# Normalising the FFN's residual from SBUF tiles, with new due times around it: an FNet + FFN kernel on one core

## The chip, the cores and the metric

One core of a Trainium2 chip runs the whole program. Time is device time in microseconds, the median of several executions. Engines are named as in the profile: PE (TensorE), DVE (VectorE), ACT (ScalarE), POOL (GpSimd) and SP (SyncE, whose queue issues most loads).

## The reference

```
x = A_x                                     # 1 x 2048 x 512
h = x + fnet(layernorm(x))                  # fnet: a = n @ hid_re.T, b = n @ hid_im.T
                                            #       y = seq_re @ a - seq_im @ b
h2 = h + silu(layernorm(h) @ w1) @ w2       # w1: 512 x 1792, w2: 1792 x 512
```

All in fp32, out 2048 x 512. The sequence matrices are 2048 x 2048, the hidden ones 512 x 512.

## The kernel before

Every fp32 product is made of three matmuls: each operand is split in a rounded part (ACT, `rounded`, L77) and a remainder (DVE, L81, written to `pl`, `gtl` and the like), and `three` (L123 to L125) adds high x high, high x low and low x high into PSUM. Four of the five large products are made with seven block products in place of eight; the sums and differences of blocks that this needs are DVE work (L411, `sums_h`, `sums_w1`, `sums_w2`, `sums_g`).

The stages follow each other on PE: `plain(0, 0)`, `fast(1, 0)`, `mix(0)` (first half q = 0: the two sequence products and the hidden one), then `fast(0, 1)`, `fast(1, 1)`, `mix(1)` for the half q = 1, then the FFN: `up(0)`, `down(0)`, `up(1)`, `down_fast(1)`. A stage `fast` is 28 steps of 12 matmuls, the first 12 of them on loaded blocks and the other 16 on differences of blocks (DVE: a subtraction L411 and a remainder L81 for each step). `mix(q)` is two halves (tau = 0, 1) of 96 matmuls; each half ends in `add_y` (L476), which adds the PSUM sums onto the tiles `h` with x, and `store_h` (L480), by which POOL writes these tiles to HBM (`hd`). `up` is steps of six matmuls, in the order n = 1, 7, 6, 2, 5 for p = 0 and then 1, 2, 3, 6, 4, 7, 5, with 3 and 4 of the p before. What follows a product there: a copy of Y to SBUF (ACT, L688, L692, L694), an add from the tile `vx` (DVE, L680) and SiLU (ACT, L677).

`norm_h(q, tau, start)` (L529) is the second layer norm, on transposed tiles, so that its sums run across partitions. Its parts have due times behind `start`: load of the residual from `hd` (-8, SP, L537), `mean` (0: two adds, then an all-reduce on POOL, L524 to L526), `center` (7 and 9, L545), `square` (10 and 12, ACT, L551), `var` (15, again `total`), `once` (21: POOL writes the row of variances to HBM, L557, and reads it back four to a partition, L559), `root` (29: thirteen small DVE operations from L563, then two DMAs on POOL, L565 and L568, that spread the result), `scale` (42 and 44, L573) and, for q = 0, `store` to HBM (46). For q = 0 the normalised tiles are loaded again (`load_hn`); `up` makes its moving side T from them, `lead` us before its start and after.

The order of all work is set by a planner: `step` counts PE's time in units of 0.2265 us per matmul (MM_US) and gives each piece of other work a due time before or behind a step; `at` gives one directly. At the end (L945) all pieces are sorted by due time, and PE, DVE, ACT and POOL each run theirs in that order. SP's transfers are issued in the order of the program too, each as soon as its page is free. Operands are rounded PREP_US = 8 before their step, loads are due LOAD_US = 18 before. All SBUF tiles but a few small ones are pages of 4 KB per partition, PAGES = 51 of them, taken and freed in turn; PSUM holds four tiles of two banks.

`down_fast(1)` ends the kernel: in the order of L894 the last product is n = 4 of p = 6, cut in two steps of three matmuls (L904 to L906), each followed by `post4` (an add, L850, and a store, L819).

At the start, 15 matmuls on zeros (WARM, L940) run on PE before the first operands are there.

Of the kernel before, what the change touches and what calls it, by code (L numbers as in the profile page):

```python
# [12 lines left out]
ALU = mybir.AluOpType  # L13
# [4 lines left out]
D = 512  # L18
# [6 lines left out]
NP = NF // 2  # L25
# [1 line left out]
NJ = S // P // 4  # L27
EPS = 1e-5
PAGES = 51
WARM = 15  # L30
MM_US = 0.2265
PREP_US = 8.0
LOAD_US = 18.0
# [5 lines left out]
def fnet_ffn_kernel(  # L39
# [20 lines left out]
    nc = tc.nc  # L60
# [7 lines left out]
    def page(name, dt=F32, shape=(2, 512)):  # L68
        return pages.tile([P, *shape], dt, tag="pg", name=name)
# [57 lines left out]
    events, clock = [], [0.0]  # L127

    def step(n, mm, before=(), after=()):

        t, end = clock[0], clock[0] + n * MM_US
        for lead, f in before:
            events.append((t - lead, 1, len(events), f))
        events.append((t, 2, len(events), mm))
        for delay, f in after:
            events.append((end + delay, 0, len(events), f))
        clock[0] = end

    def at(t, f):
        events.append((t, 1, len(events), f))  # L140
# [333 lines left out]
    def add_y(q, tau):  # L474
        for e in range(2):
            nc.vector.tensor_tensor(h[q, tau, e], y.pop((q, tau, e)), h[q, tau, e], op=ALU.add)  # L476

    def store_h(q, tau):
        for e in range(2):
            nc.gpsimd.dma_start(hd[q][tau, e], h.pop((q, tau, e)))  # L480

    def mix(q):
        for tau in range(2):
            for c in range(2):
                for i in range(2):

                    def round_h(c=c, i=i):
                        H[c, i], remainder = rounded(raw.pop(("H", c, i)), f"H{c}{i}")
                        return remainder

                    def round_c(tau=tau, c=c, i=i):
                        key = "M", q, tau, c, i
                        part[key], remainder = rounded(C.pop((c, q, i, tau)), "p", -1.0 if c else 1.0)
                        return remainder

                    def mm(tau=tau, c=c, i=i):
                        hi, lo = part.pop(("M", q, tau, c, i))
                        wh, wl = H[c, i] if tau == 0 else H.pop((c, i))
                        for e in range(4):
                            if c == 0 and i == 0 and e % 2 == 0:  # L500
                                y[q, tau, e // 2] = banks(f"y{q}{tau}{e}")
                            for m in range(2):
                                s = slice(e * P, (e + 1) * P)
                                three(y[q, tau, e // 2][:, e % 2, :], wh[:, m, s], wl[:, m, s], hi[:, m, :], lo[:, m, :],
                                      c == 0 and i == 0 and m == 0, c == 1 and i == 1 and m == 1)

                    before, after = halves(PREP_US, round_c), []
                    if tau == 0:
                        before = [(LOAD_US, lambda c=c, i=i: load_hid(c, i)), *halves(PREP_US, round_h)] + before
                    if c == 0:  # L510
                        before.append((LOAD_US - 1, lambda i=i, tau=tau: load_c(q, i, tau)))
                    if c == 1 and i == 0:
                        before.append((LOAD_US, lambda tau=tau: load_h(q, tau)))
                    if c == 1 and i == 1:
                        after = [(0, lambda tau=tau: add_y(q, tau)), (6, lambda tau=tau: store_h(q, tau))]
                    step(24, mm, before, after)

    hn = {}
    nd = dram.tile([2, 2, P, 2, 512], F32, name="nd")

    def total(a, b, name):

        t = page(name)
        nc.vector.tensor_tensor(t, a, b, op=ALU.add)  # L524
        nc.vector.tensor_tensor(t[:, 0, :], t[:, 0, :], t[:, 1, :], op=ALU.add)
        nc.gpsimd.partition_all_reduce(t[:, 1, :], t[:, 0, :], channels=P, reduce_op=REDUCE_ADD)  # L526
        return t

    def norm_h(q, tau, start):  # L529

        ln, sq = {}, {}
        token = [dram.tile([512], F32, name=f"tk{q}{tau}{n}") for n in range(2)]

        def load():
            for e in range(2):
                ln[e] = page(f"hr{q}{tau}{e}")
                nc.sync.dma_start(ln[e], hd[q][tau, e])  # L537

        def mean():
            ln["m"] = total(ln[0], ln[1], f"m{q}{tau}")  # L540

        def center(e):
            m = ln["m"]
            for n in range(2):
                nc.vector.scalar_tensor_tensor(  # L545
                    ln[e][:, n, :], m[:, 1, :], -1.0 / D, ln[e][:, n, :], op0=ALU.mult, op1=ALU.add
                )

        def square(e):
            sq[e] = page(f"sq{q}{tau}{e}")  # L550
            nc.scalar.activation(sq[e], ln[e], AF.Square)  # L551

        def var():
            ln["v"] = total(sq.pop(0), sq.pop(1), f"v{q}{tau}")

        def once():
            nc.gpsimd.dma_start(token[0], ln.pop("v")[0:1, 1, :])  # L557
            ln["w"] = small.tile([P, 4, 4], F32, name="rs2")
            nc.gpsimd.dma_start(ln["w"][:, 0, :], token[0].rearrange("(p j) -> p j", j=4))  # L559

        def root():
            v, _, _, b = w = [ln["w"][:, n, :] for n in range(4)]
            nc.vector.tensor_scalar(v, v, 1.0 / D, EPS, op0=ALU.mult, op1=ALU.add)  # L563
            guessed(*w)
            nc.gpsimd.dma_start(token[1].rearrange("(p j) -> p j", j=4), b)  # L565
            ln.pop("w")
            ln["r"] = page(f"r{q}{tau}")
            nc.gpsimd.dma_start(ln["r"][:, 0, :], token[1].partition_broadcast(P))  # L568

        def scale(e):  # L570
            v = ln.pop(e)
            for n in range(2):
                nc.vector.tensor_tensor(v[:, n, :], v[:, n, :], ln["r"][:, 0, :], op=ALU.mult)  # L573
            hn[q, e, tau] = v

        def store():
            for e in range(2):
                nc.gpsimd.dma_start(nd[tau, e], hn.pop((q, e, tau)))

        for d, f in ((-8, load), (0, mean), (7, lambda: center(0)), (9, lambda: center(1)),  # L580
                     (10, lambda: square(0)), (12, lambda: square(1)), (15, var), (21, once),
                     (29, root), (42, lambda: scale(0)), (44, lambda: scale(1))):
            at(start + d, f)
        if q == 0:
            at(start + 46, store)
# [224 lines left out]
    def down_fast(q):  # L810
# [29 lines left out]
        def mul(n, p, ms=(0, 1)):  # L840
            if p == 0:
                bank[n] = banks(f"f{n}")
            w, b = {1: (U, 0), 2: (U, 1), 3: (U, 2), 5: (V, 0), 6: (V, 1), 7: (V, 2), 4: (V, 3)}[n]
            (wh, wl), (hi, lo) = w[p], mov[n, p]
            for m in ms:
                s = slice(m * P, (m + 1) * P)
                three(bank[n][:, m, :], wh[:, b, s], wl[:, b, s], hi, lo, p == 0, p == NP - 1)
# [26 lines left out]
        def post4(m):  # L874
            add(r[1, 0][:, m, :], bank[4][:, m, :], r[1, 0][:, m, :])
            store(1, 0, m)
# [19 lines left out]
        for n, p in order:  # L896
            before, after = [], []
            if n == 6:
                before.append((LOAD_US, lambda p=p: fetch_w2(p, V, 2)))
            if n == 6 and p in (2, 3):  # L900
                before.append((LOAD_US - 1, lambda k=(1, p - 2): load_r(*k)))
            if p == NP - 1:
                after = [(0, {6: post6, 7: post7, 5: post5, 4: None}[n])]
            if n == 4 and p == NP - 1:  # L904
                for m in range(2):
                    step(3, lambda m=m: mul(4, NP - 1, (m,)), before, [(0, lambda m=m: post4(m))])  # L906
            else:
                step(6, lambda n=n, p=p: mul(n, p), before, after)

    plain(0, 0)  # L910
    for p, t in enumerate((-12, -5, 61, 68, 94, 102, 110)):
        sums_w1(clock[0] + t, p)
    fast(1, 0)
    mix(0)
    norm_h(0, 0, clock[0] - 3)
    fast(0, 1)
    norm_h(0, 1, clock[0] + 8)
    fast(1, 1)
    mix(1)
    for k in range(2):  # L920
        for tau in range(2):
            at(clock[0] - 40 + 2 * k + tau, lambda k=k, tau=tau: load_hn(k, tau))
    second = down(0), down_fast(1)
    norm_h(1, 0, clock[0] - 4)
    norm_h(1, 1, clock[0] + 15)
    up(0, 28, lambda: next(second[0]))
    list(second[0])
    up(1, 24, lambda: next(second[1]))
    list(second[1])

    warm = keep.tile([P, 512], BF16, name="warm")
# [56 lines left out]
```

## Time and profile before

| | |
|---|---|
| time, median of 3 runs | 696.88 us (696.87 to 696.95) |
| the profiled execution's own time | 696.81 us |
| its span, first to last instruction | 695.0 us |
| PE busy | 687.7 us, 3009 matmuls |
| DVE busy | 520.0 us, 666 instructions |
| ACT busy | 321.4 us, 400 instructions |
| POOL busy | 80.3 us, 99 instructions |
| moved by DMA | 160.21 MB, mean 231 GB/s |

In the rows of the timeline that follow below the columns are: start, busy time (both us), engine, line, operation, written tile <- read tiles, sizes, count, and in brackets the engine's idle time before the instruction with what ended it. A row with a count over one merges instructions that follow each other. In the waits, three numbers follow the names: us in total, times, the longest. Engine names with a q are the sequencers, which issue DMAs. Rows of DMA issues end in the KB of each and the median us from issue to landing.

### The profile page before, as it was taken

What the parts mean: (1) busy time and instruction counts of PE and PEld (TensorE: products, weight loads), DVE (VectorE), ACT (ScalarE), POOL (GpSimd) and SP (SyncE); (2) the same over time, 40 slices, a digit from 0 to 9 for tenths busy, and PEclk for the clock granted to TensorE, in tenths of its full rate; (3) what the DMA queues carried; (4) which work ended last, traced back from release to release, by engine and by line L of the source; (5) the groups of instructions that cost most, each with busy time, mean ns of one, the idle gap of its engine ahead of it and who ended that gap; (6) DMA issues with size and microseconds to landing.
All of it is one profiled execution on the core that took longest, in us unless ns stands there. A gap on an engine that the chain in (4) does not pass through costs nothing.

```text
span 695.0 us, 8349 instructions
## 1 busy us (share of the span) xinstructions
PE 687.7 (99%) x3009; PEld 563.3 (81%) x3009; DVE 520.0 (75%) x666; ACT 321.4 (46%) x400; POOL 80.3 (12%) x99
## 2 busy tenths in 40 slices
PE   9999999999999999999999999999999999999996
PEld 5788888888888888888888888887888888888885
DVE  6588975987867799899989786758797233349975
ACT  4655755434233643544364126565573045565420
POOL 1011020001013200022000023311230000000000
PEclk9999999999999999999999999999999999999999
DMA  8814369467779859687893468436996195378432
GB/s 326 309 61 156 128 219 389 168 227 235 239 236 369 333 186 339 249 299 269 282 330 123 141 219 299 129 108 206 369 407 257 35 337 215 117 267 290 121 140 91
DMA packets 54136, 160.21 MB, mean 231 GB/s; under 512 B 5968, under 2 KB 13136, under 8 KB 54096
## 3 DMA queue, kind: packets, MB, share of 16 engines
q1 hardware_dynamic: 44464, 126.11, 51.7%
q0 software_dynamic: 9632, 33.58, 12.7%
q8 instruction: 23, 0.38, 0.2%
q14 instruction: 17, 0.14, 0.1%
HBM read 122.95 MB, written 36.72 MB: 230 GB/s over the span
## 4 chain that ended last, share of the span: by engine, by line
PE 93%; DVE 3%; ACT 2%; issue 1%; DMA 0%; POOL 0%
PE m L125 11%; PE m L123 11%; PE m L124 11%; PE y L123 8%; PE y L124 8%; PE y L125 8%; PE o L124 4%; PE o L123 4%; PE o L125 4%; PE f L123 3%; PE f L125 3%; PE f L124 3%; PE c L123 3%; PE c L125 3%; PE c L124 3%; PE vx L124 2%
## 5 line engine op out<-in xcount | busy, mean ns | idle before, releaser
L77 ACT ACTIVATE ph<-raw 128x1024 fp32r<-128x1024 f32 x98 | 101.8, 1057 | 100.9 <-DVE raw L411 64.4
L81 DVE TENSOR_TENSOR pl<-raw,ph 128x1024 fp32r<-128x1024 f32 x98 | 122.3, 1260 | 23.8 <-ACT ph L77 14.0
L123 PE MATMUL m<-ph,S 128*128 128x512 f32 x192 | 74.7, 389 | 0.0
L125 PE MATMUL m<-ph,S 128*128 128x512 f32 x192 | 74.7, 389 | 0.0
L124 PE MATMUL m<-pl,S 128*128 128x512 f32 x192 | 74.7, 389 | 0.0
L411 DVE TENSOR_TENSOR raw<-raw,raw 128x1024 f32<-128x1024 f32 x48 | 60.4, 1258 | 5.3 <-DMA raw<-in_seq 5.3
L123 PE MATMUL m<-ph,X 128*128 128x512 f32 x144 | 56.0, 389 | 0.0
L124 PE MATMUL m<-pl,X 128*128 128x512 f32 x144 | 56.0, 389 | 0.0
L125 PE MATMUL m<-ph,X 128*128 128x512 f32 x144 | 56.0, 389 | 0.0
L680 DVE TENSOR_TENSOR g<-vx,cp 128x512 f32<-128x512 f32 x28 | 19.3, 689 | 39.2 <-PE vx L125 33.1
L123 PE MATMUL c<-ph,X 128*128 128x512 f32 x112 | 43.6, 391 | 0.2 <-ACT X L213 0.2
L124 PE MATMUL c<-pl,X 128*128 128x512 f32 x112 | 43.7, 390 | 0.0
L125 PE MATMUL c<-ph,X 128*128 128x512 f32 x112 | 43.6, 389 | 0.0
L124 PEld LDWEIGHTS m<-pl,S 128*128 128x128 f32 x192 | 36.0, 188 | 7.6
L125 PEld LDWEIGHTS m<-ph,S 128*128 128x128 f32 x192 | 36.0, 188 | 7.5
L123 PEld LDWEIGHTS m<-ph,S 128*128 128x128 f32 x192 | 36.0, 188 | 7.4
L677 ACT ACTIVATE g<-g 128x512 f32<-128x512 f32 x42 | 26.3, 627 | 17.4 <-DVE g L680 17.4
L123 PE MATMUL f<-gth,wf 128*128 128x512 f32 x84 | 32.9, 392 | 0.8 <-DVE r L850 0.8
L77 ACT ACTIVATE gth<-g 128x1024 fp32r<-128x1024 f32 x21 | 22.1, 1057 | 23.2 <-DVE g L838 20.7
L125 PE MATMUL f<-gth,wf 128*128 128x512 f32 x84 | 32.7, 389 | 0.0
L124 PE MATMUL f<-gtl,wf 128*128 128x512 f32 x84 | 32.7, 389 | 0.0
L123 PE MATMUL o<-ph,Uh 128*128 128x512 f32 x84 | 32.7, 389 | 0.0
(273 smaller groups left out, 1583.1 us busy)
## 6 DMA issues: line engine op xcount, KB each, us to landing
raw<-in_seq SPq DMA_DIRECT2D x98, 512.0 KB, 5.9
sf<-sd SPq DMA_DIRECT2D x28, 512.0 KB, 7.2
wf<-wd SPq DMA_DIRECT2D x28, 512.0 KB, 4.5
w<-in_ffn SPq DMA_DIRECT2D x28, 256.0 KB, 5.1
hid<-in_hid SPq DMA_DIRECT2D x8, 512.0 KB, 5.1
c<-cd SPq DMA_DIRECT2D x8, 512.0 KB, 4.9
h<-in_xT SPq DMA_DIRECT2D x8, 512.0 KB, 5.7
hd<-h POOLq DMA_DIRECT2D x8, 512.0 KB, 5.6
```

The costliest lines, as they stand in the source:

```text
L77: nc.scalar.activation(hi, src, AF.Copy, scale=sign)
L81: nc.vector.tensor_tensor(lo, src, hi, op=ALU.subtract)
L123: nc.tensor.matmul(acc, wh, mh, start=first, stop=False, skip_group_check=on)
L124: nc.tensor.matmul(acc, wh, ml, start=False, stop=False, skip_group_check=on)
L125: nc.tensor.matmul(acc, wl, mh, start=False, stop=last, skip_group_check=on)
L411: nc.vector.tensor_tensor(o, a, b, op=ALU.subtract)
L677: nc.scalar.activation(g[q, f][:, tau, :], src, AF.Silu)
L680: nc.vector.tensor_tensor(g[q, f][:, tau, :], src, other, op=ALU.add)
```

## The change

1. `norm_h` loses its load. Its mean and its centering read the tiles `h` in which `add_y` made the sum; the centering writes new pages. `store_h` keeps the tiles (the end of the kernel still reads `hd`) and is due 0.5 behind `add_y` instead of 6.
2. `norm_h(q, tau)` is called at the end of each half of `mix(q)`, with `start` 2 us behind that half. Before, the starts were: (0, 0) 3 us ahead of the end of `mix(0)`, (0, 1) 8 us behind the end of `fast(0, 1)`, (1, 0) 4 us ahead of and (1, 1) 15 us behind the end of `mix(1)`.
3. The moving side T of the first FFN layer is made with a lead of 44 and 64 us instead of 28 and 24, its loads 60 us ahead of the end of `mix(1)` instead of 40. The seven `sums_w1` have other times.
4. The last product is one step of six matmuls, with both `post4` behind it.
5. WARM is 13 instead of 15.

```diff
-WARM = 15
+WARM = 13
...
     def store_h(q, tau):
         for e in range(2):
-            nc.gpsimd.dma_start(hd[q][tau, e], h.pop((q, tau, e)))
+            nc.gpsimd.dma_start(hd[q][tau, e], h[q, tau, e])
...
                     if c == 1 and i == 1:
-                        after = [(0, lambda tau=tau: add_y(q, tau)), (6, lambda tau=tau: store_h(q, tau))]
+                        after = [(0, lambda tau=tau: add_y(q, tau)), (0.5, lambda tau=tau: store_h(q, tau))]
                     step(24, mm, before, after)
+            norm_h(q, tau, clock[0] + 2)
...
-        def load():
-            for e in range(2):
-                ln[e] = page(f"hr{q}{tau}{e}")
-                nc.sync.dma_start(ln[e], hd[q][tau, e])
-
         def mean():
-            ln["m"] = total(ln[0], ln[1], f"m{q}{tau}")
+            ln["m"] = total(h[q, tau, 0], h[q, tau, 1], f"m{q}{tau}")

         def center(e):
-            m = ln["m"]
+            src, m = h.pop((q, tau, e)), ln["m"]
+            ln[e] = page(f"hr{q}{tau}{e}")
             for n in range(2):
                 nc.vector.scalar_tensor_tensor(
-                    ln[e][:, n, :], m[:, 1, :], -1.0 / D, ln[e][:, n, :], op0=ALU.mult, op1=ALU.add
+                    ln[e][:, n, :], m[:, 1, :], -1.0 / D, src[:, n, :], op0=ALU.mult, op1=ALU.add
                 )
...
-        for d, f in ((-8, load), (0, mean), (7, lambda: center(0)), (9, lambda: center(1)),
+        for d, f in ((0, mean), (7, lambda: center(0)), (9, lambda: center(1)),
...
             if p == NP - 1:
-                after = [(0, {6: post6, 7: post7, 5: post5, 4: None}[n])]
-            if n == 4 and p == NP - 1:
-                for m in range(2):
-                    step(3, lambda m=m: mul(4, NP - 1, (m,)), before, [(0, lambda m=m: post4(m))])
-            else:
-                step(6, lambda n=n, p=p: mul(n, p), before, after)
+                after = [(0, {6: post6, 7: post7, 5: post5}.get(n))]
+                if n == 4:
+                    after = [(0, lambda m=m: post4(m)) for m in range(2)]
+            step(6, lambda n=n, p=p: mul(n, p), before, after)

     plain(0, 0)
-    for p, t in enumerate((-12, -5, 61, 68, 94, 102, 110)):
+    for p, t in enumerate((-24, -12, -5, 30, 61, 68, 88)):
         sums_w1(clock[0] + t, p)
     fast(1, 0)
     mix(0)
-    norm_h(0, 0, clock[0] - 3)
     fast(0, 1)
-    norm_h(0, 1, clock[0] + 8)
     fast(1, 1)
     mix(1)
     for k in range(2):
         for tau in range(2):
-            at(clock[0] - 40 + 2 * k + tau, lambda k=k, tau=tau: load_hn(k, tau))
+            at(clock[0] - 60 + 2 * k + tau, lambda k=k, tau=tau: load_hn(k, tau))
     second = down(0), down_fast(1)
-    norm_h(1, 0, clock[0] - 4)
-    norm_h(1, 1, clock[0] + 15)
-    up(0, 28, lambda: next(second[0]))
+    up(0, 44, lambda: next(second[0]))
     list(second[0])
-    up(1, 24, lambda: next(second[1]))
+    up(1, 64, lambda: next(second[1]))
     list(second[1])
```

## The prediction

> **What bounds the kernel now.** I read the page first, then the waits of TensorE (PE), then the timeline of every engine around each place where PE waits.
>
> ```profile
> span 695.0 us, 8349 instructions
> PE 687.7 (99%) x3009; PEld 563.3 (81%) x3009; DVE 520.0 (75%) x666; ACT 321.4 (46%) x400; POOL 80.3 (12%) x99
> ```
>
> PE is busy all the time, so only its pace and its few gaps count. These are all its waits on work of the kernel (times: total, count, longest); the row after them is the wait of SP's queue that the change takes away:
>
> ```profile
> PE f L123 <- DVE r L850: 0.8, 1, 0.8
> PE y L123 <- ACT cp L692: 0.4, 1, 0.4
> PE vx L123 <- DVE g L680: 0.2, 1, 0.2
> PE c L123 <- ACT X L213: 0.2, 1, 0.2
> ```
> ```profile
> SPq L537 <- DMA hd<-h: 44.2, 6, 23.1
> ```
>
> A step of six matmuls takes 1.36 us start to start (425.28 to 426.64, two PE rows quoted below), 0.2267 each. The 2994 matmuls behind the warm-up need 2994 x 0.2267 = 678.7; they begin at 7.49 (quoted below), so without a gap the last would end its turn at 686.2. In the trace it starts at 690.12 and ends its turn at 690.35. **Some 4 us of PE time is all that any change of waits can win**, and part of it lies in the first microseconds. The 44 us that SP's queue stands still for the written residual end in no wait of PE: operands are rounded 8 us ahead of their step (PREP_US), and that covers the late loads. I price their going at 0.
>
> **The last two tiles in one step.** PE, then DVE, at the end:
>
> ```profile
> 688.38 0.39 PE L125 MATMUL f<-gth,wf 128*128 128x512 f32 x1
> 689.55 0.50 PE L123 MATMUL f<-gth,wf 128*128 128x512 f32 x1 [0.78 <-DVE r L850]
> 690.12 0.40 PE L125 MATMUL f<-gth,wf 128*128 128x512 f32 x1
> ```
> ```profile
> 688.80 0.69 DVE L850 TENSOR_TENSOR r<-f,r 128x512 f32<-128x512 f32 x1 [1.04 <-PE f L125]
> 690.55 0.69 DVE L850 TENSOR_TENSOR r<-f,r 128x512 f32<-128x512 f32 x1 [1.06 <-PE f L125]
> ```
>
> The second half's first matmul waits for the add that reads the other half of the same PSUM tile: the whole tile is the unit of waiting. In one step it starts at 688.61 and the last one at 689.07, **1.05 sooner**. Both adds then stand behind the last matmul, one more than now, 0.6 (two of this size on DVE start 0.6 apart). Net **-0.45**. Ends: -1.05, if the first add still ran beside PE; 0, if the two stores, now issued 0.6 apart and not 1.75, cost each other that much.
>
> **The two waits in the first layer go.** Here are they, and what DVE does at that time:
>
> ```profile
> 473.29 0.50 PE L123 MATMUL vx<-T7h,sf 128*128 128x512 f32 x1 [0.24 <-DVE g L680]
> 475.38 0.50 PE L123 MATMUL y<-T5h,sf 128*128 128x512 f32 x1 [0.43 <-ACT cp L692]
> ```
> ```profile
> 471.35 1.28 DVE L573 TENSOR_TENSOR hr<-hr,r 128x512 f32<-128x512 f32 x2
> 472.55 0.68 DVE L680 TENSOR_TENSOR g<-vx,cp 128x512 f32<-128x512 f32 x1
> ```
>
> L573 is the scaling of norm_h(1, 1), in DVE's order ahead of the add that PE waits for. It is due 13 us sooner after the change, so the add ends 1.2 sooner and both waits go. A wait costs its idle time, plus 0.16 (a matmul is busy 0.39 but the next one starts after 0.23), plus 0.1 for the next start: 0.24 + 0.43 + 2 x 0.26 = **-1.2** (0, if other work fills the place).
>
> The T tiles made sooner cure no wait of PE: 0. The earlier sums_w1 put the same DVE, ACT and POOL work elsewhere, again where operands stand 8 us ahead: 0. By my count of first and last uses, at most 50 of the 51 pages are taken (49 now), in fast(0, 1); loads into pages issue later there: 0, upper end +1.
>
> **norm_h sooner brings a new wait.** Its load goes and no DMA takes its place; the hd stores remain, as the end of the kernel reads them. But norm_h(q, 1) now begins 2 us behind mix(q), and norm_h(q, 0) half a mix earlier, 96 x 0.2265 = 21.7. POOL runs in the order of due times; counted from the end of mix it gets: hd stores (+0.5), `once` of (q, 0) (-21.7 + 2 + 21 = +1.3), all-reduce of the mean of (q, 1) (+2). `once` is two DMAs, and the second waits for the first to land, while POOL stands:
>
> ```profile
> 413.41 0.53 POOL L480 DMA_DIRECT2D hd<-h  x1 [1.95 <-DVE h L476]
> 428.35 3.23 POOL L526 PARTITION_ALL_REDUCE m<-m  x1 [0.90 <-DVE m L525]
> 431.46 0.50 POOL L557 DMA_DIRECT2D tk<-v  x1
> 434.47 0.58 POOL L559 DMA_DIRECT2D rs<-tk  x1 [2.50 <-DMA tk<-v]
> ```
> ```profile
> 237.57 0.53 POOL L557 DMA_DIRECT2D tk<-v  x1 [0.29 <-POOL v L526]
> 243.07 0.59 POOL L559 DMA_DIRECT2D rs<-tk  x1 [4.97 <-DMA tk<-v]
> ```
> ```profile
> 413.95 3.60 SPq L537 DMA_DIRECT2D hr<-hd  x2
> ```
>
> So the all-reduce gets 3.6 us (first layer) or 6.1 us (second fast stage) ahead of it. DVE, in order, then stands at the centering; behind that are `root` of (q, 0), thirteen small operations, and PE's operands.
>
> **In up(0)**, from 411.7 on (425.28 is its eleventh step: less 10 x 1.36), the due times behind the start are centering +9, root +9.26, and the add of n = 2, p = 1 +9.51. The rows now, DVE, ACT, PE, and root from an earlier stage:
>
> ```profile
> 421.47 0.69 DVE L680 TENSOR_TENSOR g<-vx,cp 128x512 f32<-128x512 f32 x1 [0.55 <-PE vx L125]
> 431.93 1.28 DVE L545 SCALAR_TENSOR_TENSOR hr<-m,hr 128x512 f32<-128x512 f32 x2
> ```
> ```profile
> 423.26 0.62 ACT L677 ACTIVATE g<-g 128x512 f32<-128x512 f32 x1
> 424.12 0.60 ACT L692 ACTIVATE cp<-y 128x512 f32<-128x512 f32 x1 [0.24 <-PE y L125]
> 436.27 1.04 ACT L551 ACTIVATE sq<-hr 128x1024 f32<-128x1024 f32 x1
> ```
> ```profile
> 425.28 0.39 PE L123 MATMUL vx<-T7h,sf 128*128 128x512 f32 x1
> 426.64 0.39 PE L123 MATMUL y<-T5h,sf 128*128 128x512 f32 x1
> ```
> ```profile
> 247.52 0.16 DVE L563 TENSOR_SCALAR rs<-rs 128x4 f32<-128x4 f32 x1
> 249.99 1.23 DVE L81 TENSOR_TENSOR pl<-raw,ph 128x1024 fp32r<-128x1024 f32 x1
> ```
>
> The last hd store is issued by 413.9, the token's first DMA by 414.4. It lands 2.5 later, and not before the store ahead of it in the queue, whose readback SP could issue at about 417.2 (413.95 + 3.60, less one issue): 417.3. The second DMA 0.6, the all-reduce 3.2: 421.1. Centering starts 0.4 behind that (431.93 against 428.35 + 3.23) and takes 1.2, root 2.5 (247.52 to 249.99), the add 0.7: **425.9 instead of 422.2**. PE's n = 7 writes the tile that this add reads and could start at 425.28: 0.7 late, 0.1 to start again. ACT then does silu, the square and the copy of Y, 0.55 + 0.95 + 0.6: 428.05; n = 5 waits for that copy and would start at 426.64 + 0.8 = 427.4: 0.6 + 0.1. Together **+1.5**. Ends: 0, if the all-reduce is not held up; +3.5, if the all-reduce takes the 4.06 quoted next and add_y itself is 1.2 late behind the one before it.
>
> **In fast(0, 1)**, 864 matmuls, 195.9 us, before up(0), so from 215.8 on, the chain is the same. How full DVE is, and what happens beside an all-reduce:
>
> ```profile
> 226.00:274.00 48.00, 48.00 (x213) 39.69 (x212) 43.13 (x52) 23.52 (x26) 7.87 (x8) 1.00 0.76 281
> ```
> ```profile
> 232.96 4.40 DVE L81 TENSOR_TENSOR pl<-raw,ph 128x1024 fp32r<-128x1024 f32 x2
> ```
> ```profile
> 233.22 4.06 POOL L526 PARTITION_ALL_REDUCE v<-v  x1 [8.54 <-DVE v L525]
> ```
> ```profile
> 251.41 0.39 PE L124 MATMUL m<-pl,S 128*128 128x512 f32 x1
> ```
> ```profile
> rs<-tk POOLq DMA_DIRECT2D x4, 2.0 KB, 2.9
> ```
>
> In the first row the third pair of columns is DVE: 43.13 of 48 us busy. The remainder that DVE writes from 249.99 to 251.22 is read at 251.41: **0.2 us to spare**. And of the two remainders beside the all-reduce one took some 3.2 us instead of 1.2. With the change add_y ends at 217.3 (1.5 into the stage, as in up(0)); hd 0.8, token 0.5 + 5.0 + 0.6, all-reduce 4.1: 228.2. Centering, root, centering and a remainder (6.1) end at 234.3; that remainder is due 8 us before step 7 and read by its second matmul, at 215.8 + 7 x 2.72 + 0.23 = 235.1: no wait. Three remainders and the variance (5.3) start the second all-reduce at 238.5; until 242.6 it holds DVE, then its own `once` (6.1) and the landing of rs (2.9 by the median of the four; at most 4.4, as root at 247.52 did not wait; I take 4) put root of (0, 1) at 252.8 to 255.3. A subtraction and a remainder (2.3) end at 257.6; read at 256.8: **+0.8**. Ends: 0; +3.5, if the token waits 2.4 longer behind the hd stores, which makes every later link later. fast(1, 1), which loses this work, had no wait to lose.
>
> The Trainium skill, page "SBUF — State Buffer", section "Who interferes with whom", says that a VectorE instruction with two SBUF inputs and a GpSimd one that reads SBUF shut each other out for a whole instruction; the row at 232.96 agrees, and by the rule the two all-reduces that move into this stage could hold DVE 8 us in place of my 2 or so, which would give rival 2's time.
>
> **Two warm-up matmuls fewer.**
>
> ```profile
> 1.18 6.35 PE L941 MATMUL idle<-warm 128*128 128x512 bf16 x15 [1.18 <-DVE warm L932]
> 7.49 0.99 PE L310 MATMUL c<-ph,X 128*128 128x512 f32 x2
> ```
> ```profile
> 6.83 1.10 ACT L195 ACTIVATE X<-x,rs 128x256 fp32r<-128x256 f32 x2 [1.97 <-DVE rs L179]
> ```
>
> ACT's first X tile ends half way through its pair, at 7.38: PE starts with its data, not with the end of the warm-up. 0; ends -0.05 and rival 3.
>
> **Sum**, on the profiled execution's 696.81 (span 695.0 and 1.81 around it; the median of the three runs is 0.07 more, which changes nothing): -0.45 - 1.2 + 1.5 + 0.8 = +0.65, so **697.5**. From 696.88, 0.2% (1.4 us) is about what a measurement tells from no change.
>
> **Rivals.** 1, faster: POOL's token lands early and DVE reaches the adds in time. 696.81 - 1.65 = 695.2, and hardly less, since no other wait of PE is touched. For it: `once` holds POOL only 3.6 us in the first layer; against it: the due times that put root ahead of the add. 2, slower: the all-reduce of the mean of (0, 1) ends later than 229.0 (0.8 after my 228.2), from where on each delay goes to PE in full. With both upper ends 3.5 + 3.5 - 1.65 gives 702.2, with two thirds of them 699.8, which I take. For it: 43.1 of 48, 0.2 to spare; against it: DVE makes up 0.45 in each step of 2.72 (a pair of operations takes 2.27). 3, slower: with 0.85 us of warm-up gone PE's full pace comes later. A warm-up matmul takes 0.42, a later one 0.23; a delay of 0 to the warm-up's own 6.35 us costs 0 to 3.0. I take 1.5: 699.0. The Trainium skill, page "TensorE: Matmul & The Clock Gate", section "Part 1: The HAM clock gate (the "warmup" mystery)", has windows of 3.4 us in which PE must be busy; one more of them at the low rate would cost 1.6; no run here shows a window.
>
> **Chances.** Forecast 0.44, its own range 696.0 to 698.6; rival 1 0.19; rival 2 0.32; rival 3 0.05. The range reaches to rival 1 and over most of rival 2: 695.1 to 701.2. Below 695.5 lies rival 1: faster 0.19. Above 698.3 lie rivals 2 and 3 and a seventh of the forecast: slower 0.43. Within: 0.38.
>
> **What would show it.** Right: `once` ahead of a mean's all-reduce on POOL; DVE idle ahead of L545; waits of PE on L680 and L692 some 14 us into up(0), none at 473, none on L850 at the end. Wrong: no new wait of PE at all (rival 1); m matmuls waiting for L81 in fast(0, 1) (rival 2); starts 0.42 apart behind 7.49 (rival 3).

## The result, and the profile after

| | before | after |
|---|---|---|
| time, median | 696.82 us (17 runs) | 698.48 us (17 runs) |
| profiled execution | 696.81 | 698.38 |
| its span | 695.0 | 696.2 |
| time outside the span | 1.81 | 2.18 |

The ratio of after to before is 1.0027, with a 95% interval of 1.002 to 1.0035: 1.7 us **slower**. Predicted were 697.5, in a range of 695.1 to 701.2.

The page of the kernel after, its span and busy times:

```profile
span 696.2 us, 8332 instructions
PE 687.3 (99%) x3007; PEld 563.1 (81%) x3007; DVE 518.6 (74%) x666; ACT 320.2 (46%) x400; POOL 79.0 (11%) x99
```

The busy shares say nothing of the loss; PE's list of waits does. Kernel after, all waits of PE (total, count, longest); lines 677 and 689 are 680 and 692 of before:

```profile
PE vx L123 <- DVE g L677: 1.4, 1, 1.4
PE idle L932 <- DVE warm L923: 1.2, 1, 1.2
PE y L123 <- ACT cp L689: 0.4, 1, 0.4
PE c L310 <- ACT X L195: 0.4, 1, 0.4
PE c L123 <- ACT X L213: 0.2, 1, 0.2
```

The wait on the last add (L850) is gone. The waits on the add and the copy look like those of before, but they are others: they stand at 427, not at 473. Kernel after, timeline, PE and then ACT:

```profile
425.29 0.39 PE L125 MATMUL vx<-T4h,wal 128*128 128x512 f32 x1
427.05 0.50 PE L123 MATMUL vx<-T7h,sf 128*128 128x512 f32 x1 [1.37 <-DVE g L677]
...
429.14 0.50 PE L123 MATMUL y<-T5h,sf 128*128 128x512 f32 x1 [0.42 <-ACT cp L689]
```
```profile
427.02 0.63 ACT L674 ACTIVATE g<-g 128x512 f32<-128x512 f32 x1 [3.43 <-DVE g L677]
427.56 1.05 ACT L548 ACTIVATE sq<-hr 128x1024 f32<-128x1024 f32 x1
428.51 0.58 ACT L689 ACTIVATE cp<-y 128x512 f32<-128x512 f32 x1
```

A matmul without a wait starts 0.2267 behind the one ahead of it. By that measure the two starts lose 1.53 and 0.58, and the matmul behind each of them 0.11: **2.33 us**. Now what the add waited for. The same place on DVE and on POOL:

```profile
422.62 1.29 DVE L542 SCALAR_TENSOR_TENSOR hr<-m,h 128x512 f32<-128x512 f32 x2 [0.22 <-POOL m L527]
423.84 0.16 DVE L560 TENSOR_SCALAR rs<-rs 128x4 f32<-128x4 f32 x1
...
426.30 0.69 DVE L677 TENSOR_TENSOR g<-vx,cp 128x512 f32<-128x512 f32 x1
```
```profile
410.35 3.72 POOL L527 PARTITION_ALL_REDUCE v<-v  x1 [11.55 <-DVE v L526]
413.94 1.08 POOL L480 DMA_DIRECT2D hd<-h  x2
415.01 0.50 POOL L554 DMA_DIRECT2D tk<-v  x1
418.80 0.58 POOL L556 DMA_DIRECT2D rs<-tk  x1 [3.28 <-DMA tk<-v]
419.41 3.18 POOL L527 PARTITION_ALL_REDUCE m<-m  x1
```

Read upwards from the add: it starts when the thirteen operations of the root are through (423.84 to 426.30), these follow the first centering (422.62), that waits for the all-reduce of the mean of (1, 1) (419.41), and the all-reduce stands on POOL behind the second DMA of the token of (1, 0), which waits 3.28 for the first DMA to land. This is the chain that the prediction described, with one link that it did not have: the all-reduce of the variance of (1, 0) starts at 410.35 and keeps even the two stores of h until 413.94.

In fast(0, 1), DVE and the PE row that it holds up (kernel after, timeline):

```profile
226.58 1.30 DVE L542 SCALAR_TENSOR_TENSOR hr<-m,h 128x512 f32<-128x512 f32 x2 [3.20 <-POOL m L527]
...
237.34 3.17 DVE L81 TENSOR_TENSOR pl<-raw,ph 128x1024 fp32r<-128x1024 f32 x1 [0.34 <-PE m L124]
...
251.93 0.16 DVE L560 TENSOR_SCALAR rs<-rs 128x4 f32<-128x4 f32 x1
...
255.53 1.22 DVE L81 TENSOR_TENSOR pl<-raw,ph 128x1024 fp32r<-128x1024 f32 x1
```
```profile
256.35 0.39 PE L123 MATMUL m<-ph,X 128*128 128x512 f32 x1
256.81 0.50 PE L124 MATMUL m<-pl,X 128*128 128x512 f32 x1
```

The remainder ends at 256.75, the matmul that reads it starts at 256.81 and not at 256.58. With 0.11 behind it and 0.11 at 270.9 the stage loses 0.45. The remainder at 237.34, which alone takes 1.22, took 3.17 beside an all-reduce.

At the end (kernel after, PE's last matmul and the two adds behind it):

```profile
690.51 0.39 PE L125 MATMUL f<-gth,wf 128*128 128x512 f32 x1
```
```profile
690.94 1.29 DVE L847 TENSOR_TENSOR r<-f,r 128x512 f32<-128x512 f32 x2 [1.72 <-PE f L125]
```

The span ends 5.66 us behind the start of that matmul, 4.93 before: 0.73 given back of the 1.06 that the half step had cost PE.

In the two profiled executions the parts make +2.33 + 0.45 - 1.22 (the waits at 473, gone) - 0.33 (the end) = +1.23. The first product starts 0.28 sooner (7.21, not 7.49) and the matmuls that wait for nothing take 0.2 more in all, which leaves some 1.15; the spans, as rounded, differ by 1.2. Another 0.4 lies **outside the span**, where no step of the prediction stood.

### The profile page after: what moved, and what is told of

It is laid out like the page before. It is cut to its first block, busy times and chain, and to the rows that moved or that the text cites. A ratio compares the mean times of both kernels' runs of the same rounds, so it can differ in the third digit from the quotient of the medians.

```text
span 696.2 us, 8332 instructions
## 1 busy us (share of the span) xinstructions
PE 687.3 (99%) x3007; PEld 563.1 (81%) x3007; DVE 518.6 (74%) x666; ACT 320.2 (46%) x400; POOL 79.0 (11%) x99
## 4 chain that ended last, share of the span: by engine, by line
PE 53%; DVE 8%; issue 2%; DMA 1%; POOL 1%; ACT 1%; DVEq 0%; SPq 0%; POOLq 0%; ACTq 0%
PE m L124 5%; PE m L125 5%; PE m L123 5%; PE o L124 4%; PE o L125 4%; PE o L123 4%; PE y L123 3%; PE y L125 3%; PE y L124 3%; PE f L123 3%; PE f L124 3%; PE f L125 3%; PE vx L123 2%; PE vx L124 2%; PE vx L125 2%
## 5 line engine op out<-in xcount | busy, mean ns | idle before, releaser
L81 DVE TENSOR_TENSOR pl<-raw,ph 128x1024 fp32r<-128x1024 f32 x98 | 120.3, 1241 | 27.9 <-ACT ph L77 20.0
L411 DVE TENSOR_TENSOR raw<-raw,raw 128x1024 f32<-128x1024 f32 x48 | 58.6, 1221 | 0.3 <-DMA raw<-in_seq 0.3
```

The costliest lines, as they stand in the source:

```text
L81: nc.vector.tensor_tensor(lo, src, hi, op=ALU.subtract)
L411: nc.vector.tensor_tensor(o, a, b, op=ALU.subtract)
```

## The experiments

Ten kernels, all timed in five rounds beside the kernel before on the same chip; its median was 696.71 beside the first four, 696.74 beside the next four, 696.66 beside the last two. The table has medians; before's span is 694.9 and the rest 1.78 beside each of the three groups, so that the chip does not set it.

| kernel | time | ratio to before (95%) | span | outside |
|---|---|---|---|---|
| after | 698.48 | 1.0027 (1.002 to 1.0035) | 696.3 | 2.21 |
| tail_only | 696.51 | 0.9997 (0.9988 to 1.0006) | 694.7 | 1.77 |
| tiles_only | 696.80 | 1.0000 (0.9992 to 1.0009) | 694.8 | 2.00 |
| lead_only | 696.94 | 1.0004 (0.9995 to 1.0013) | 695.0 | 1.96 |
| warm15 | 698.47 | 1.0026 (1.0016 to 1.0036) | 696.2 | 2.20 |
| q1_old | 697.03 | 1.0011 (1.0002 to 1.0020) | 695.2 | 1.85 |
| root_late | 695.81 | 0.9987 (0.9978 to 0.9996) | 693.8 | 1.98 |
| once_late | 698.49 | 1.0030 (1.0019 to 1.0041) | 696.3 | 2.21 |
| q0_old | 695.49 | 0.9982 (0.9973 to 0.9991) | 693.4 | 2.07 |
| both_late | 695.29 | 0.9982 (0.9973 to 0.9991) | 693.4 | 1.87 |
| tail_cover | 694.45 | 0.9972 (0.9960 to 0.9984) | 692.6 | 1.87 |

The time outside the span keeps within 0.08 of its median in one kernel's runs and differs between kernels by up to 0.44. So the spans are the sharper measure of what a wait costs, and they are used below.

**Theory:** the loss is DVE's order in up(0) (root ahead of the add, both behind a late all-reduce), and a smaller one of the same kind in fast(0, 1). **Rivals:** the all-reduce alone, whatever stands behind it; the longer lead of the T tiles; the warm-up; the pages.

### tail_only: the last two tiles in one step, alone

The kernel before with the diff's edit of the last product (n = 4, p = 6).

> The kernel before with one edit: the last two output tiles in one step. Two things are open. In the trace of the kernel after, the span ends 5.66 us behind the start of the last matmul, before 4.93: 0.73 more, where I had priced 0.6, and the last matmul itself should start 1.05 sooner. And the time outside the span is 2.2 us in the runs of after and was 1.81 in the one run of before whose span I have: 0.4 that no step of mine foresaw. Theory 1: the tail as I priced it, with the larger 0.73: span 695.0 - 0.3 = 694.7 and the time 0.3 below the kernel before; time outside the span stays 1.8. Theory 2: the tail carries the 0.4 outside the span as well, because two stores end together: span 694.7, time outside 2.2, and the time the same as before to 0.1. Rival: the first of the two adds still runs beside the last matmuls and the gain is the whole 1.05.

Span 694.7, time 0.20 less than before, outside 1.77. Theory 1 holds, and the first add does not run beside PE, whose last matmul starts at 689.49 (kernel tail_only, timeline of DVE):

```profile
689.92 1.29 DVE L850 TENSOR_TENSOR r<-f,r 128x512 f32<-128x512 f32 x2 [1.72 <-PE f L125]
```

Both adds start behind the last matmul. The tail is worth 0.2 us and carries nothing of the time outside.

The execution that was profiled is the slowest of the eleven (697.02, span 695.3), and its trace has a wait that before's has not. It stands in fast(1, 1), where the start times of before put the second norm of q = 0 (kernel tail_only, timeline of DVE, then PE):

```profile
334.96 0.17 DVE L563 TENSOR_SCALAR rs<-rs 128x4 f32<-128x4 f32 x1 [3.10 <-DMA rs<-tk]
```
```profile
338.71 0.50 PE L124 MATMUL m<-pl,S 128*128 128x512 f32 x1 [0.16 <-DVE pl L81]
```

The root waits for its token until 334.96, the remainder behind it comes late, and PE loses 0.43. So the old start times can cost something too, when a token lands late.

### tiles_only: the readback removed, alone

```diff
-                nc.sync.dma_start(ln[e], hd[q][tau, e])
...
-            ln["m"] = total(ln[0], ln[1], f"m{q}{tau}")
+            ln["m"] = total(h[q, tau, 0], h[q, tau, 1], f"m{q}{tau}")
```

with the centering from h as in the change, and every start time of before.

> The kernel before with the first part of the change alone: the mean and the centering of norm_h read the tiles of h in SBUF, the readback from HBM goes, and every start time stays as it was before. I priced the removed waits of SP (44.2 us) at 0. Theory: no wait of PE moves; time within 0.15 of the kernel before (696.7), HBM reads 4.19 MB less, SP's wait on hd gone. Rival 1: SP's queue, free sooner, brings operands earlier and the small waits at 473 shrink: up to 1.2 faster. Rival 2: h pages held until the centering press the 51 pages, loads wait, and it is slower by 0.5 or more.

696.80 beside 696.74: no difference. SP's 44.2 us of waiting are gone, and PE's list is that of before but for its waits in the first microseconds (kernel tiles_only; lines 846 and 688 are the last add and the copy):

```profile
PE f L123 <- DVE r L846: 0.8, 1, 0.8
PE y L123 <- ACT cp L688: 0.4, 1, 0.4
PE vx L123 <- DVE g L676: 0.2, 1, 0.2
```

What gives the change its name moves the time by nothing.

### lead_only: the T tiles and sums_w1 sooner, alone

```diff
-    for p, t in enumerate((-12, -5, 61, 68, 94, 102, 110)):
+    for p, t in enumerate((-24, -12, -5, 30, 61, 68, 88)):
...
-            at(clock[0] - 40 + 2 * k + tau, lambda k=k, tau=tau: load_hn(k, tau))
+            at(clock[0] - 60 + 2 * k + tau, lambda k=k, tau=tau: load_hn(k, tau))
...
-    up(0, 28, lambda: next(second[0]))
+    up(0, 44, lambda: next(second[0]))
...
-    up(1, 24, lambda: next(second[1]))
+    up(1, 64, lambda: next(second[1]))
```

> The kernel before with the third part of the change alone: the T tiles of both layers made sooner (leads 44 and 64 instead of 28 and 24), the earlier sums of w1 and the load of the first half's norm 60 us ahead instead of 40. I priced it at 0. Theory: no wait of PE goes or comes, time within 0.15 of the kernel before (696.7), the waits at 473 of 0.4 and 0.6 as before. Rival: the T tiles hold pages sooner, loads of the mix wait for pages, and it is 0.5 or more slower. Rival 2: the sooner T tiles leave DVE freer at 471 to 473 and the two waits shrink: up to 1.2 faster.

Span 695.0 against 694.9, time 696.94 against 696.66 (the interval holds 1): PE's losses at 473 are 0.40 and 0.61 as before, no wait is gone. The 0.28 in the time is above the 0.15 that I gave, and 0.17 of it is time outside the span. Neither rival holds.

### warm15: the kernel after with 15 warm-up matmuls

```diff
-WARM = 13
+WARM = 15
```

> The kernel after with its 15 warm-up matmuls back. The first product starts at 7.21 in the trace of after, 7.49 before, because the first load landed 0.28 sooner, and the time outside the span is 0.4 longer. Theory 1: the two matmuls do nothing to the time (they end before the data come), and the 0.28 is the scatter of a load; time within 0.1 of after's 698.4. Theory 2: the number of warm-up instructions shifts where the span begins against the launch: with 15 the start is back at 7.49 and the time outside at 1.8, and the sum of the two is the same. Rival: fewer warm-up matmuls slow the first products down by themselves; then 15 makes the kernel 0.3 or more faster than after.

The same time as after (698.47 and 698.48) and the same time outside (2.20 and 2.21). The first product starts at 7.39 here, between 7.19 and 7.47 in the seven profiles with 13 and between 7.26 and 7.49 in the five with 15: it scatters, whatever the number of warm-up matmuls. Theory 1 holds.

### q1_old: the norms of q = 1 back at their old times

```diff
-            norm_h(q, tau, clock[0] + 2)
+            if q == 0:
+                norm_h(q, tau, clock[0] + 2)
...
+    norm_h(1, 0, clock[0] - 4)
+    norm_h(1, 1, clock[0] + 15)
     up(0, 44, lambda: next(second[0]))
```

> The kernel after with the two norms of q = 1 at the start times that they had before (4 us ahead of the end of the mix and 15 behind it), still from the tiles in SBUF. Theory: the waits of PE at 427 and 429 (2.33) go, because the token of (1, 0) and the all-reduce of (1, 1) come in another order, and the two waits at 473 (1.22) come back: span 696.2 - 1.1 = 695.1, time 697.3. What is left of fast(0, 1), about 0.45, stays. Rival: the readback that went was what made the place at 473 late, not the due time of the scaling; then the waits at 473 do not come back and the time is 696.1. Rival 2: the longer lead of the T tiles (44 instead of 28) makes the waits at 427 on its own; then they stay and the time is 699 or more.

Span 695.2, 1.1 under after, as expected; the time 697.03, 0.3 under the 697.3 expected, which is time outside. The waits are those of before again, on copy and add, and with them a matmul of fast(0, 1) (kernel q1_old):

```profile
PE y L123 <- ACT cp L690: 0.4, 1, 0.4
PE vx L123 <- DVE g L678: 0.2, 1, 0.2
...
PE m L124 <- DVE pl L81: 0.2, 1, 0.2
```

They stand at 473 and 475 (0.40 and 0.60 lost, 0.11 behind each): the due time of the scaling made them, not the readback. The waits at 427 are gone although the T tiles keep their lead of 44, so rival 2 is out.

### root_late: the root of q = 1 behind the add

```diff
-                     (29, root), (42, lambda: scale(0)), (44, lambda: scale(1))):
+                     (29 + 5 * q, root), (42 + 8 * q, lambda: scale(0)), (44 + 8 * q, lambda: scale(1))):
```

> The kernel after with one edit for the first layer's second norm (q = 1): the root is due 5 us later, the scaling 8 us later, so that the add of n = 2 stands ahead of the root of (1, 0) in DVE's order. The chain of POOL (token, its wait, then the all-reduce) is left as it is. Theory: the add waits only for the centering, which ends at 423.84 in the trace of after, and ends at 424.5, before PE needs its tile at 425.28; the waits of PE at 427.05 and 429.14 go, 2.33 us in all, and with the 473 waits still gone the span is 693.9, the time 2.3 below after (696.1), 0.7 below before. Rival 1: DVE is late at this place whatever the order, because the all-reduce held it; then a wait of 0.5 us or more stays on the add. Rival 2: the ACT square ahead of the copy of Y keeps its own wait of about 0.6; then 1.5 of the 2.3 go. Rival 3: the root, put later, meets the adds of n = 4 and n = 5, and a new wait of 1 us or more appears some 3 to 6 us further on.

Span 693.8, 2.5 under after and as expected; the time is 695.81, **faster than both**, and 0.3 below the 696.1 expected, most of it outside the span (1.98 against 2.21). Kernel root_late, DVE and PE at the place:

```profile
423.01 1.29 DVE L542 SCALAR_TENSOR_TENSOR hr<-m,h 128x512 f32<-128x512 f32 x2 [0.21 <-POOL m L527]
424.22 0.68 DVE L677 TENSOR_TENSOR g<-vx,cp 128x512 f32<-128x512 f32 x1
424.82 1.28 DVE L542 SCALAR_TENSOR_TENSOR hr<-m,h 128x512 f32<-128x512 f32 x2
...
426.69 0.16 DVE L560 TENSOR_SCALAR rs<-rs 128x4 f32<-128x4 f32 x1
```
```profile
425.65 0.39 PE L125 MATMUL vx<-T4h,wal 128*128 128x512 f32 x1
425.88 0.39 PE L123 MATMUL vx<-T7h,sf 128*128 128x512 f32 x1
```

The all-reduce is as late as in after (the centering still waits for it, until 423.01), and yet PE goes on in step: the add, ahead of the root, ends at 424.9. Both waits are gone and none has come in their place in up(0), which speaks against all three rivals.

### once_late: the all-reduce first, the root where it was

```diff
-                     (10, lambda: square(0)), (12, lambda: square(1)), (15, var), (21, once),
+                     (10, lambda: square(0)), (12, lambda: square(1)), (15, var), (21 + 2 * q, once),
```

> The kernel after with one edit: for q = 1 the token (once) is due 2 us later, so that on POOL the all-reduce of the mean of (1, 1) comes ahead of the token of (1, 0); the root keeps its place on DVE, ahead of the add of n = 2. Theory: the stall has two parts, the late all-reduce and the root ahead of the add. This edit cures the first and makes the second worse: the all-reduce runs from 415.7 to about 419, the centering follows at 419 to 420 and not at 422.6; the token's first DMA is issued at 419.5, lands 2.5 later, the second lands 2.9 to 4.4 behind its issue, so the root begins at 425.5 to 427 and ends 2.5 later; the add ends at 428.7 to 430.1, PE's n = 7 (425.3) is 3.4 to 4.8 late. Time 1.2 to 2.8 above after: 699.6 to 701.3. Rival: the late all-reduce alone made the stall; with it first in line the waits at 427 and 429 go and the time is 696.1.

698.49, as after: the rival's 696.1 is refuted, but so is my size. Kernel once_late, POOL and DVE:

```profile
415.73 3.23 POOL L527 PARTITION_ALL_REDUCE m<-m  x1 [0.51 <-DVE m L526]
418.83 0.50 POOL L554 DMA_DIRECT2D tk<-v  x1
420.68 0.58 POOL L556 DMA_DIRECT2D rs<-tk  x1 [1.35 <-DMA tk<-v]
```
```profile
421.22 1.29 DVE L542 SCALAR_TENSOR_TENSOR hr<-m,h 128x512 f32<-128x512 f32 x2
424.16 0.17 DVE L560 TENSOR_SCALAR rs<-rs 128x4 f32<-128x4 f32 x1 [1.65 <-DMA rs<-tk]
...
426.63 0.69 DVE L677 TENSOR_TENSOR g<-vx,cp 128x512 f32<-128x512 f32 x1
```

The all-reduce comes 3.7 us sooner and the centering no longer waits. The root, still ahead of the add, now waits 1.65 for its own token and starts at 424.16 instead of 423.84. The token was issued 0.7 sooner than I had taken (418.83, not 419.5) and landed 1.85 behind that (420.68) where I had taken 2.5; hence no worse than after. So there are two ways in which the root comes late, and curing one hands over to the other: **the place of the root decides.**

### q0_old and both_late: the wait in fast(0, 1)

q0_old is root_late with norm_h(0, 0) at 3 us ahead of the end of mix(0) and norm_h(0, 1) at 8 us behind fast(0, 1), as before:

```diff
-            norm_h(q, tau, clock[0] + 2)
+            if q == 1:
+                norm_h(q, tau, clock[0] + 2)
...
     mix(0)
+    norm_h(0, 0, clock[0] - 3)
     fast(0, 1)
+    norm_h(0, 1, clock[0] + 8)
```

> root_late with the two norms of q = 0 back at the start times that they had before (3 us ahead of the end of the mix, and 8 us behind the end of the second fast stage), still from the tiles in SBUF, which (0, 1) now holds through the whole of fast(0, 1). In the trace of root_late a remainder ends late in fast(0, 1) and PE loses 0.55 + 0.11 + 0.10 there; in that of after it was 0.45, in that of warm15 0.2, and with the old times none in that place. Theory: the second norm's DVE and POOL work in fast(0, 1) makes this wait; it goes, 0.3 to 0.7 less than root_late's 695.8: 695.1 to 695.5. Rival 1: two more pages held for 80 us make loads late in fast(0, 1): 0.5 or more slower than root_late. Rival 2: the work meets a like place in fast(1, 1) and costs there what it cost here: 695.8.

both_late keeps the norms in fast(0, 1) and puts root and scaling later there too (the edit against the kernel after):

```diff
-                     (29, root), (42, lambda: scale(0)), (44, lambda: scale(1))):
+                     (34, root), (50, lambda: scale(0)), (52, lambda: scale(1))):
             at(start + d, f)
         if q == 0:
-            at(start + 46, store)
+            at(start + 54, store)
```

> root_late with the same edit for q = 0 too: there the root is due 5 us later, the scaling and the store 8 us later. In the trace of root_late DVE works without a break from 232 to 260, and the root of (0, 1), 252.26 to 254.72, stands ahead of a subtraction and the remainder that PE waits for (ends 257.08). Theory: each step of 2.72 us in this stage has two operations of 1.13 to 1.2 each, so DVE makes up about 0.4 a step; a root and scalings 2 to 3 steps later meet a smaller lag, and the wait of 0.6 to 0.7 shrinks to 0.2 or less: time 695.2 to 695.5. Rival 1: the lag at that place is set by the all-reduce and not by the root's place, and the scalings put later add their own: the same 695.8. Rival 2: the longer hold of four pages presses the 51 pages: slower.

Both times lie in the ranges given. Both have a span of 693.4, 0.4 under root_late, whose wait in fast(0, 1) had cost 0.76 in its profile (0.45 in that of after, 0.19 in that of warm15: it scatters). Neither has a wait there in its profile. All waits of PE in both_late:

```profile
PE c L310 <- ACT X L195: 1.9, 1, 1.9
PE idle L932 <- DVE warm L923: 1.2, 1, 1.2
PE c L123 <- ACT X L213: 0.2, 1, 0.2
```

Only waits of the first 31 us are left. Taking the work out of the stage and putting its root 5 us later in it are worth the same, so the amount of work in the stage does not make the wait by itself; with the root in another place it is gone. That pages press was not seen in either.

### tail_cover: both_late, with cover for the add at the end

```diff
-        order += [(n, p) for n in (6, 7, 5, 4) for p in range(4, NP)]
-        for n, p in order:
+        order = [(n, p, (0,) if n == 4 and 0 < p < 4 else (0, 1)) for n, p in order]
+        late4 = range(4, NP)
+        order += [(n, p, (0, 1)) for n in (6, 7) for p in late4] + [(4, p, (0,)) for p in late4]
+        order += [(5, p, (0, 1)) for p in late4] + [(4, p, (1,)) for p in range(1, NP)]
+        for n, p, ms in order:
...
-                    after = [(0, lambda m=m: post4(m)) for m in range(2)]
-            step(6, lambda n=n, p=p: mul(n, p), before, after)
+                    after = [(0, lambda m=m: post4(m)) for m in ms]
+            step(3 * len(ms), lambda n=n, p=p, ms=ms: mul(n, p, ms), before, after)
```

> both_late with the last layer's end in another order: the first half of the product n = 4 is finished ahead of the product n = 5, whose 18 matmuls lie between the add that reads that half and the first matmul that writes the other half of the same tile; the second half (18 matmuls, p = 1 to 6) comes last. The number of matmuls is the same. Reading to be tested: the half step of the kernel before cost PE 1.05 because nothing lay between the add and the next matmul of its tile, and the single step costs one more add behind the last matmul instead. With a cover of 4.1 us neither is paid: PE's last matmul at the same place as in both_late (687.74), one add of 0.69 behind it and not two, the end 0.6 sooner: span 692.8 and, with the time outside the span between 1.8 and 2.2 as in the runs so far, 694.6 to 695.0. Rival: the two large stores of n = 5 are still under way and hold the last one up, so that the end comes no sooner: span 693.4. Rival 2: PE waits again, on the adds of n = 7 that stand ahead of the first half's add on DVE.

Time 694.45, span 692.6, 0.8 under both_late. Kernel tail_cover, DVE and PE at the end:

```profile
681.51 0.68 DVE L847 TENSOR_TENSOR r<-f,r 128x512 f32<-128x512 f32 x1
...
688.17 0.69 DVE L847 TENSOR_TENSOR r<-f,r 128x512 f32<-128x512 f32 x1 [1.72 <-PE f L125]
```
```profile
687.75 0.39 PE L125 MATMUL f<-gth,wf 128*128 128x512 f32 x1
```

The first half's add runs at 681.5 under the matmuls of n = 5, PE ends where it ended in both_late (687.74), and one add remains: 0.6, as expected, and 0.2 more. One store goes out behind the last matmul here and two in both_late; that the store is worth the 0.2 is not shown. This version beats the kernel before by 2.2 us, a ratio of 0.9972 (0.996 to 0.9984).

## Why the prediction was right, and where its sizes were not

The mechanism was the forecast's own: `once` of (1, 0) ahead of the all-reduce on POOL, root ahead of the add on DVE, waits on L680 and L692 of before some 14 us into up(0), none left at 473 or at the end. The sum was +0.65 and the medians say +1.66. By its point the forecast expected a change too small to be told from none; the time fell only just into its own 696.0 to 698.6. The 1.0 that is missing is mostly up(0) (0.83) and the time outside the span (0.43), less 0.35 in fast(0, 1), and that these errors partly cancel is luck. Step by step:

- **New waits in up(0): 1.5 predicted, 2.33 measured.** This is the term that was mis-sized. I had POOL free for the stores of h at 413.4; the all-reduce of the variance of (1, 0), which DVE's adds release only at 410.35, holds it until 413.94. And the token's landing, taken as 2.9 behind its issue, took 3.8 (415.01 to 418.80), and 3.8 in each of the other five kernels that issue it there right behind the two stores. The all-reduce of the mean came 1.5 later than reckoned; its end and the centering made up 0.4 of that, and PE was 0.24 later at its place (425.29 + 0.23, not 425.28). root_late and once_late show that the root's place ahead of the add is what turns this into a wait of PE.
- **fast(0, 1): 0.8 predicted, 0.45 in the profile of after,** 0.19 to 0.76 in others, 0.4 in the medians (root_late against both_late). The all-reduce of the mean of (0, 1) ended at 226.5, not at 228.2. Rival 2, with its later token, did not come. That fast(1, 1), which loses this work, had no wait to lose holds for before's profile, but not for tail_only's (0.43). By the rule of the Trainium skill that I set beside it (page "SBUF — State Buffer", section "Who interferes with whom") the two all-reduces were to cost DVE some 8 us; the trace agrees in that the one remainder that met an all-reduce was held, but by some 2 us (3.17 instead of 1.22) and not by the all-reduce's whole 3.23, and the other all-reduce found DVE waiting for it anyway.
- **The waits at 473: -1.2 predicted, -1.22 measured,** and q1_old, which brings the old due times back, brings them back.
- **The tail: -0.45 predicted, -0.33 in the profile, -0.2 in the medians of tail_only.** The second add was priced at 0.6; behind the last matmul came 0.73. In tail_cover, with one add and one store there, the span ends 4.83 behind the last matmul's start and not 5.66; how much of the difference is the store stays open.
- **The removed readback, the sooner T tiles and the warm-up: 0 each,** and 0 in tiles_only, lead_only and warm15 as far as spans go (-0.1, +0.1 and 0). Rival 3 is refuted. The Trainium skill's windows of the clock gate (page "TensorE: Matmul & The Clock Gate", section "Part 1: The HAM clock gate (the "warmup" mystery)") would, by the estimate that I gave with it, have made two warm-up matmuls cost 1.6; no run here shows such a cost. Thirteen warm-up matmuls take 5.63 in after, all 0.43 apart, and 4.29 in both_late, where the later ones start 0.22 apart; in both the products from the third on start about 0.23 apart, so the full pace was there in time.
- **Time outside the span: not in the sum, +0.43 measured** (1.78 to 2.21). It is a quarter of the result. It does not go with the tail (1.77) or with the warm-up (2.20); tiles_only (2.00), lead_only (1.96) and q1_old (1.85) each have a part of it, and root_late, which has after's instructions in another order, has 1.98. The traces show nothing of it, and its cause stays open.

The spans add up: 694.9 before, -0.2 (tail), -0.1 and +0.1 (tiles, leads), +0.4 (norms of q = 0, root_late against q0_old), +1.1 (norms of q = 1, from q1_old to after) = 696.2, against 696.3 measured.

## What to carry to other kernels

When work is moved in an order that engines keep strictly, look at what stands directly ahead of the operations that the bounding engine waits for: here thirteen tiny operations in the wrong place cost 2.3 us, while 44 us of waiting on an engine's queue and 4.2 MB of reads cost nothing. To size such a stall, follow each queue back until it is known to be idle; one all-reduce further up made 0.6 of the 1.5 us by which the token was late. And where an add keeps PE from its tile, put another product's matmuls between them, rather than join the steps and pay the add at the end.

## What the runs showed of the hardware

- The landing of the same small DMA (the token, 2 KB) as POOL sees it, issue to next issue, scatters widely. Right behind stores of 0.5 MB it takes 3.8 in up(0) (3.78 to 3.80 in six kernels) and 3.76 to 5.70 in fast(0, 1), where after has 4.95:

```profile
217.80 0.53 POOL L554 DMA_DIRECT2D tk<-v  x1
222.75 0.59 POOL L556 DMA_DIRECT2D rs<-tk  x1 [4.41 <-DMA tk<-v]
```

  With no store just ahead of it in POOL's queue it takes 1.85 (once_late), but also 3.01 and 5.50 (the two rows of before that the prediction shows) and 6.38 (tail_only, 322.98 to 329.36). So stores ahead of it are not the only thing that makes it late; what else does, these runs do not separate.

- The time outside the span belongs to the program: 1.77 to 2.21 in twelve kernels, within 0.08 of the median in the runs of any one. Differences of 0.2 us between two kernels can lie there, where no row of the trace explains them.
